# A four-layer attention kernel: hand-assigned buffers, strided layer B weights, norms on ScalarE and a moved overflow check

## The chip, the cores and the metric

The program runs on one core of a Trainium2 chip. The metric is the device time of one execution in microseconds, as the median of several runs. One execution of each kernel is also recorded by the hardware profiler; all profile lines below come from such a record. Engines are named as in the profile: PE (TensorE matmul) with PEld (its weight loads), DVE (VectorE), ACT (ScalarE), POOL (GpSimd) and SP (SyncE, which issues nearly all transfers here).

## The reference

Input is a sequence of 2048 tokens with 512 features in bf16. Four residual layers follow each other, A, B, A, B, each `x = x + layer(layernorm(x))`, with 32 heads of 16 features. Both A layers share their weights, and so do both B layers.

```python
# layer A: linear attention
pq, pk = q @ w_phi, k @ w_phi                    # per head, 16 x 16
phi_q = concat(softmax(pq), softmax(-pq))        # phi_k from pk likewise
kv = einsum("bhsf,bhsd->bhfd", phi_k, v); z = phi_k.sum(s)
o = (phi_q @ kv) / (phi_q @ z + 1e-6)
out = o @ wo
# layer B: each token looks at 8 tokens, 0, 2, .. 14 positions back
logits = q . k[pos - 2 * w] * 16 ** -0.5         # masked ahead of the start
o = softmax(logits) @ v[pos - 2 * w]
out = o @ wo
```

## The kernel before, in words

Tokens lie on partitions for the normalization and in blocks of 512 (b = 0 to 3) on the free axis elsewhere. x stays in SBUF through all layers, as four tiles of 128 x 4 x 512. `w_phi` is folded into the q and k weights at the start (`s_fold`, WA).

**Normalization.** Mean and variance come from `bn_stats` for the first layer (L379) and later from sums that the residual step leaves behind: the residual is added either on PE, by one more matmul with the identity (L411), and copied out by ACT (L418), or on DVE (L421); ACT squares x for the sum of squares (L428). DVE applies the normalization (L334, `xn`), PE transposes (L348), ACT or DVE copies out (`xnT`, L146 or L148).

**Layer A.** `s_a1`: k and v by matmul (L469, L481), exp of k and -k on ACT (L475, `Ek`), sums over features as a tree on DVE (L501, L505, L509, L513), reciprocals on ACT, one multiplication on DVE (L521), and the sum over tokens on PE (L530). `s_a2`: q (L559) and its exps (L565, `Eq`). `s_akv`, `s_a3`, `s_a4`: the masked kv matrices (L600, L607), denominators, a broadcast of rho either by PE (L654, L660) or by a round trip through DRAM (L669, L676, L680), the product (L705) and the output projection with the residual (`s_out`, L408).

**Layer B.** `s_b1` computes q, k, v with features as rows and tokens as columns (L727), four groups c of 128 features for each. In these groups each head's features are split over the four groups, so the columns of the weights are taken in the order (h, dl) for each c. Before, GpSimd makes a permuted copy WB of the raw weights for it (L278). ACT or DVE copies the results out (K, QT, V). V is spread by transfers from SBUF to SBUF into `Vg` (L779): 16 for each block. `s_b2`: products of q with eight shifted views of k on DVE (L808, `prod`), sums over features by PE (L815), exps on ACT (L822, `E`, whose row sums go into `stE`), denominators (L831, L836, L838, `rden`, sums into `stR`) and the normalized weights (L843, `PT`). `s_b3`: products with the shifted v on DVE (L868, `pav`), sums by PE (L875), output projection (L408) and residual. In the last layer the result is stored from there (L432).

**The check.** The exps are taken without a maximum. Whether this is safe is checked: norms of the folded weights (`s_bound`: squares on GpSimd L300, column sums on PE L305, comparison and count on DVE L309), the sums in `stE` and `stR` (L893, L895), all added up over partitions by PE (L900) and compared on DVE (L902, L904). Every engine loads the result `fl` (L906) and branches over a second, general program (L1541) that is there for the case that it isn't safe; it is not run here.

**Order and buffers.** Each engine works through its queue in order. The queues' order is written out by hand: `_ORDER` is a table of base-36 numbers, each naming a thread (a stage and an engine), and `run()` takes the next step of that thread. `_CHOICE` has a digit for each step that can run on either of two engines (which engine copies out; whether the residual is added on PE). Tiles come from pools: `big` with 8 buffers (Ek, Vg, prod, pav), `med` with 16 (xn, xnT, Eq, K, QT, V, oT and others), `t2` with 6, and `ps` with 8 PSUM banks. A pool hands its buffers out in turn, so a new tile waits until the tile that had the buffer has been read for the last time.

## Time and profile before

| what | value |
|---|---|
| median of 3 runs | 368.34 us (368.2 to 368.52) |
| the profiled execution's own time | 368.67 us |
| its span, first to last instruction | 367.0 us |
| mean granted TensorE clock | 0.989 |
| GpSimd busy | 18.8 us |
| transfers | 30.65 MB, mean 84 GB/s |

The profile is read in this way: the page gives busy time and share of the span for each engine; a group line gives source line, engine, operation, tiles written <- read, shapes and count, then busy us and mean ns, then the idle time of the engine before these instructions and what ended it. A timeline line gives start and duration in us of a run of like instructions, and in brackets the idle time before it. A chain line gives start, duration and what the end of the program was waiting for. A line of a single source line gives durations in ns as minimum/median/maximum and the first and the last start. Durations of matmuls are modelled and overlap, so PE is judged by the distance between starts.

### The profile page before, as it was taken

To read this page: it belongs to the slowest core of one execution; us is meant where nothing else is said; L and a number is where in the kernel's file an instruction comes from. 1 tells how busy PE (TensorE), PEld (TensorE's weight loads), DVE (VectorE), ACT (ScalarE), POOL (GpSimd) and SP (SyncE) were. 2 spreads that over 40 slices of the span, in tenths; PEclk is the share of its full clock that TensorE was granted. 3 is DMA by queue.
4 is the path that set the end of the run, shared out by engine and by line. 5 is a ranking of instruction groups with operands and counts; after the bars stand their busy time and mean duration, and the time that the engine had idled before them with its cause. 6 is when DMAs were issued, how large, how long until landed. Compare 5 with 4: busy or idle time off the path is not lost.

```text
span 367.0 us, 7333 instructions
## 1 busy us (share of the span) xinstructions
PE 336.5 (92%) x2868; PEld 162.5 (44%) x2868; DVE 318.5 (87%) x460; ACT 272.9 (74%) x622; POOL 18.8 (5%) x40
## 2 busy tenths in 40 slices
PE   1999899899999999999997999997999999998591
PEld 0645456644544443443433556643454444433130
DVE  7689987699689999999997959797799999995972
ACT  2579798487866979789897998487678889775250
POOL 3070400300000000000000000000000000000000
PEclk9999999999999999999999999999999999999897
DMA  7930000013400799309940000015204796489513
GB/s 232 350 94 0 3 0 2 4 46 92 110 1 0 125 152 158 55 29 174 189 84 0 2 0 3 2 51 133 65 0 85 134 158 97 91 157 167 118 53 127
DMA packets 17242, 30.65 MB, mean 84 GB/s; under 512 B 4272, under 2 KB 11952, under 8 KB 17200
## 3 DMA queue, kind: packets, MB, share of 16 engines
q1 hardware_dynamic: 16672, 30.09, 39.6%
q8 instruction: 24, 0.39, 0.5%
q14 instruction: 18, 0.15, 0.2%
q10 hardware_dynamic: 528, 0.02, 0.1%
HBM read 10.50 MB, written 2.36 MB: 35 GB/s over the span
## 4 chain that ended last, share of the span: by engine, by line
PE 64%; DVE 16%; ACT 9%; DMA 6%; issue 2%; SPq 1%; DVEq 0%; ACTq 0%
PE ps L727 23%; PE ps L408 13%; PE ps L815 4%; PE ps L481 4%; PE ps L348 4%; PE ps L875 3%; ACT Ek L475 3%; DMA Vg<-V 3%; PE ps L705 3%; PE ps L469 3%; DVE Ek L521 2%; ACT Eq L565 2%; DVE pav L868 2%; PE ps L530 2%; DVE Eq L660 2%
## 5 line engine op out<-in xcount | busy, mean ns | idle before, releaser
L727 PE MATMUL ps<-xnT,WB 128*128 128x512 bf16 x384 | 88.0, 379 | 0.0
L808 DVE TENSOR_TENSOR prod<-QT,K 128x4096 bf16<-128x4096 bf16 x32 | 72.0, 2288 | 2.1 <-ACT K L148 1.7
L868 DVE TENSOR_TENSOR pav<-PT,Vg 128x4096 bf16<-128x4096 bf16 x32 | 71.4, 2288 | 0.3
L727 PEld LDWEIGHTS <-WB 128*128 128x128 bf16 x384 | 36.4, 98 | 48.0 <-issue 5.9
L148 ACT CAST oT<-ps 128x512 bf16<-128x512 f32 x58 | 33.1, 602 | 17.6 <-PE ps L875 11.5
L408 PEld LDWEIGHTS <-oT 128*128 128x128 bf16 x256 | 23.8, 99 | 33.7 <-issue 7.4
L475 ACT ACTIVATE Ek<-ps 128x512 bf16<-128x512 f32 x64 | 34.5, 625 | 3.3 <-PE ps L469 3.3
L565 ACT ACTIVATE Eq<-ps 128x512 bf16<-128x512 f32 x64 | 34.1, 632 | 2.5 <-PE ps L559 1.5
L408 PE MATMUL ps<-WoB,oT 128*128 128x512 bf16 x128 | 32.7, 390 | 0.0
L469 PE MATMUL ps<-WA,xnT 128*128 128x512 bf16 x128 | 31.1, 379 | 1.6 <-DVE vaug L146 1.3
L481 PE MATMUL ps<-WA,xnT 128*128 128x512 bf16 x128 | 32.0, 390 | 0.0
L408 PE MATMUL ps<-WoA,oT 128*128 128x512 bf16 x128 | 31.3, 380 | 0.0
L559 PE MATMUL ps<-xnT,WA 128*128 128x512 bf16 x128 | 30.5, 379 | 0.2 <-ACT Eq L565 0.2
L428 ACT ACTIVATE sqd<-x 128x512 bf16<-128x512 bf16 x48 | 30.0, 632 | 0.8 <-DVE x L421 0.5
L421 DVE SCALAR_TENSOR_TENSOR x<-ps,x 128x512 bf16<-128x512 f32 x37 | 24.4, 685 | 5.8 <-PE ps L408 5.7
L348 PE MATMUL ps<-ident,xn 128*128 128x128 bf16 x256 | 19.7, 225 | 8.4 <-DVE xn L334 8.4
L875 PE MATMUL ps<-pav,indAV 128*32 128x512 bf16 x256 | 18.9, 391 | 7.0 <-DVE pav L868 5.2
L148 ACT COPY xnT<-ps 128x1024 bf16<-128x1024 bf16 x21 | 21.1, 1035 | 3.3 <-PE ps L348 3.3
L348 PEld LDWEIGHTS <-xn 128*128 128x128 bf16 x256 | 16.6, 100 | 15.4 <-DVE xn L334 10.0
L521 DVE TENSOR_TENSOR Ek<-Ek,rk 128x4096 bf16<-128x4096 bf16 x8 | 18.3, 2289 | 5.5 <-ACT rk L518 5.5
L148 ACT CAST QT<-ps 128x512 bf16<-128x512 f32 x30 | 17.5, 586 | 5.6 <-PE ps L727 5.3
L418 ACT ACTIVATE x<-ps 128x512 bf16<-128x512 f32 x27 | 15.8, 598 | 7.6 <-PE ps L411 7.4
(118 smaller groups left out, 468.3 us busy)
## 6 DMA issues: line engine op xcount, KB each, us to landing
Vg<-V SPq DMA_DIRECT2D x128, 131.5 KB, 4.7
Prho<-rd SPq DMA_DIRECT2D x8, 512.0 KB, 4.7
out_dram<-x SPq DMA_DIRECT2D x8, 256.0 KB, 2.5
x<-in_A_x_dram SPq DMA_DIRECT2D x3, 512.0 KB, 8.3
wbraw<-in_B_wqkv_dram SPq DMA_DIRECT2D x3, 512.0 KB, 8.8
wraw<-in_A_wqkv_dram SPq DMA_DIRECT2D x2, 512.0 KB, 6.4
x<-in_A_x_dram SPq DMA_DIRECT2D x4, 128.0 KB, 2.5
WA<-in_A_wqkv_dram SPq DMA_DIRECT2D x1, 512.0 KB, 4.4
```

Of the source, the lines that this page charges most:

```text
L148: self.nc.scalar.copy(out=out, in_=in_)
L348: nc.tensor.transpose(U["pt", t // 2][:, (t % 2 * NB + c) * P:(t % 2 * NB + c + 1) * P], self.xn[key, b][:, t, c * P:(c + 1) * P], self.id ...
L408: nc.tensor.matmul(y[:], lhsT=oT[:, c, t * P:(t + 1) * P], rhs=Wo()[:, c, :], start=(c == 0), stop=(c == NB - 1 and not onpe))
L428: nc.scalar.activation(out=sqd[:], in_=xb[:, t, :], func=ACT.Square, accum_out=T["ss"][:, t:t + 1])
L469: nc.tensor.matmul(pk[:], lhsT=xnT[:, t, k, :], rhs=self.WA[:, k, D:2 * D], start=(k == 0), stop=(k == NB - 1))
L475: nc.scalar.activation(out=T["E"][:, t, s, :], in_=T["k", t][:], func=ACT.Exp, scale=1.0 - 2.0 * s)
L481: nc.tensor.matmul(pv[:], lhsT=xnT[:, t, k, :], rhs=self.WA[:, k, 2 * D:3 * D], start=(k == 0), stop=(k == NB - 1))
L559: nc.tensor.matmul(pq[:], lhsT=self.WA[:, k, hb * P:(hb + 1) * P], rhs=xnT[:, :, k, :], start=(k == 0), stop=(k == NB - 1))
L565: nc.scalar.activation(out=self.Eq[L, b][s][:, :, hb, :], in_=T[hb][:].rearrange("p (t i) -> p t i", t=4), func=ACT.Exp, scale=1.0 - 2.0 * s)
L727: nc.tensor.matmul(pp[:], lhsT=self.WB[:, k, i, c, :], rhs=xnT[:, :, k, :], start=(k == 0), stop=(k == NB - 1))
L808: nc.vector.tensor_tensor(out=pr[:], in0=QT[:, c:c + 1, :].to_broadcast([P, NW, TB]), in1=win, op=ALU.mult)
L868: nc.vector.tensor_tensor(out=pv[:], in0=PT[:].unsqueeze(1).to_broadcast([P, NB, 2, TB]), in1=vw, op=ALU.mult)
```

## The change

It has four parts, and with them both tables are written anew.

1. **Buffers by hand.** Each pool is split into pools of one buffer, and `_SLOTS` names the buffer of every tile in the order in which tiles are made. The numbers of buffers stay 8, 16, 6 and 8. `wT` and the two tiles of `Eq` are made one step later.
2. **Layer B's weights.** WB is loaded as it lies in DRAM; group c takes every fourth column from c on. The rows of WoB are loaded in the matching order, in runs of one row where they were runs of four. GpSimd's twelve copies are gone.
3. **Weight norms.** ACT squares the q and k parts of WA with a running sum (one sum for each partition); GpSimd's squares, PE's eight matmuls and DVE's two counts are gone. The bound is now on the sum over the whole matrix.
4. **The flag.** It becomes three scheduled steps: counts (DVE), total (PE), decide (DVE), with a sign and a threshold for each of four numbers; the load of `fl` by every engine stays at the end.

`_ORDER` and `_CHOICE` are new, so that nearly every queue differs; by the built queues PE adds 21 residuals, where it added 27.

```diff
-COLN2_MAX = 3.0
+FRO2_MAX = 2.9
+_BUFS = {"big": 8, "med": 16, "t2": 6, "ps": 8}
 _ORDER = """
-4 1r 4 0 5 4 0 1 4 4 6 6 0 0 2 0 2 3 n o n 7 16 16 p n q n r n n t 15 8 8 8 8 16 16 1a u u s 13 8 19 9 8 8 8 8
+0 8l 0 4 4 1f 1 n 4 0 0 n 0 5 4 o 2 4 6 6 p n 2 n q u 3 u n n t 8 8 8 8 9 15 15 s 16 7 15 w 8 15 8 8 8 9i 17 v
...
+_SLOTS = {
+    "big": (
+        "01234567012437437561327546107534610751205462034162034571620345712630416325725472014751432"
+    ),
...
-        self.bigp = e(tc.tile_pool(name="bigp", bufs=8))
+        self.bigp = e(tc.tile_pool(name="bigp", bufs=1))
...
+    def slot(self, kind):
+        k = self.ntile[kind]
+        self.ntile[kind] = k + 1
+        return kind + _SLOTS[kind][k]
...
-        return self.bigp.tile([P] + shape, BF16, name=name, tag="big")
+        return self.bigp.tile([P] + shape, BF16, name=name, tag=self.slot("big"))
...
-        self.WB = const.tile([P, NB, 3, NB, P], BF16, name="WB")
+        self.WB = const.tile([P, NB, 3 * D], BF16, name="WB")
...
         def ld(i):
-            T[i] = self.med([NB, D], "wbraw")
-            nc.sync.dma_start(out=T[i][:], in_=wbv[:, :, i * D:(i + 1) * D])
-
-        def cp(i, m):
-            nc.gpsimd.tensor_copy(
-                out=self.WB[:, m, i, :, :].rearrange("p c (h dl) -> p c h dl", dl=4),
-                in_=T[i][:, m, :].rearrange("p (h c dl) -> p c h dl", c=NB, dl=4))
+            wbv = self.B_wqkv.rearrange("(m p) c -> p m c", p=P)
+            nc.sync.dma_start(out=self.WB[:, :, i * D:(i + 1) * D], in_=wbv[:, :, i * D:(i + 1) * D])
 
         def wo(c):
-            wo_v = self.B_wo.rearrange("(h c q) n -> c h q n", c=NB, q=4)
+            wo_v = self.B_wo.rearrange("(h q c) n -> c h q n", c=NB, q=4)
...
         def sq(qk):
-            T[qk] = self.med([NB, D], "sq")
-            w = self.WA[:, :, qk * D:(qk + 1) * D]
-            nc.gpsimd.tensor_tensor(out=T[qk][:], in0=w, in1=w, op=ALU.mult)
-
-        def mm(qk):
-            T["p", qk] = pn = self.ps()
-            for m in range(NB):
-                nc.tensor.matmul(pn[:], lhsT=self.ones[:], rhs=T[qk][:, m, :], start=(m == 0), stop=(m == NB - 1))
-
-        def cmp(qk):
-            okm = self.t2([D], "okm")
-            nc.vector.tensor_scalar(out=okm[:], in0=T["p", qk][:], scalar1=COLN2_MAX, scalar2=None,
-                                    op0=ALU.is_le, op1=ALU.add, accum_out=self.okc[:, qk:qk + 1])
+            junk = self.med([NB, D], "sq")
+            nc.scalar.activation(out=junk[:], in_=self.WA[:, :, qk * D:(qk + 1) * D], func=ACT.Square,
+                                 accum_out=self.okc[:, qk:qk + 1])
...
-                nc.tensor.matmul(pp[:], lhsT=self.WB[:, k, i, c, :], rhs=xnT[:, :, k, :],
+                nc.tensor.matmul(pp[:], lhsT=self.WB[:, k, i * D + c:(i + 1) * D:NB], rhs=xnT[:, :, k, :],
...
+    def s_flag(self):
+        nc, add = self.nc, self.step
+        T = {}
+
+        def counts():
+            junk = self.sm([24], "junk", F32, 1)
+            nc.vector.tensor_scalar(out=junk[:, 0:16], in0=self.stE[:], scalar1=SUM_E_MAX, scalar2=None,
+                                    op0=ALU.is_le, op1=ALU.add, accum_out=self.okc[:, 2:3])
+            nc.vector.tensor_scalar(out=junk[:, 16:24], in0=self.stR[:], scalar1=SUM_R_MAX, scalar2=None,
+                                    op0=ALU.is_le, op1=ALU.add, accum_out=self.okc[:, 3:4])
+            T["okb"] = self.sm([4], "okb", BF16, 1)
+            nc.vector.tensor_tensor(out=T["okb"][:], in0=self.okc[:], in1=self.sgn[:], op=ALU.mult)
+
+        def total():
+            T["p"] = self.ps()
+            nc.tensor.matmul(T["p"][:, 0:4], lhsT=self.ones[:], rhs=T["okb"][:], start=True, stop=True)
+
+        def decide():
+            ok = self.sm([4], "ok", F32, 1)
+            nc.vector.tensor_tensor(out=ok[:], in0=T["p"][:, 0:4], in1=self.thr[:], op=ALU.is_ge)
+            tot = self.sm([1], "tot", F32, 1)
+            nc.vector.tensor_reduce(out=tot[:], in_=ok[:], axis=AX.X, op=ALU.add)
+            self.fl = self.sm([1], "fl", I32, 1)
+            nc.vector.tensor_scalar(out=self.fl[:], in0=tot[:], scalar1=4.0, scalar2=None, op0=ALU.not_equal)
+
+        add("flag", "DVE", counts)
+        add("flag", "PE", total)
+        add("flag", "DVE", decide)
```

Line numbers of the changed kernel are higher: 13 more in the norms and transposes (L334 becomes L347, L421 becomes L434), 15 more in layer B (L727 becomes L742, L808 becomes L823, L868 becomes L883), and 29 more for the helper that copies (L146 becomes L175, L148 becomes L177).

149 lines of the change are left out of this document (76 added, 73 removed).

## The prediction, made before the changed kernel ran

> **What bounds the kernel now.** I read the page first, then busy time by stage, then the DVE timeline, the chain of waits and single source lines where something stood out. The page gives the length and the load of each engine:
>
> ```profile
> span 367.0 us, 7333 instructions
> PE 336.5 (92%) x2868; PEld 162.5 (44%) x2868; DVE 318.5 (87%) x460; ACT 272.9 (74%) x622; POOL 18.8 (5%) x40
> ```
>
> Two engines near 90% can be one bottleneck or two that take turns. The busy time by stage (columns: stretch, its length, then PE, PEld, DVE, ACT, POOL busy us with counts) tells:
>
> ```profile
> 20.00:82.00 62.00, 58.31 (x692) 33.53 (x690) 53.83 (x91) 49.09 (x106) 12.62 (x14) 1.00 0.04 10
> 82.00:110.00 28.00, 28.00 (x155) 13.57 (x154) 23.41 (x49) 20.30 (x46) 0.32 (x2) 1.00 0.28 72
> 110.00:200.00 90.00, 88.16 (x629) 37.38 (x628) 87.87 (x98) 75.70 (x178) 0.79 (x4) 1.00 0.58 98
> 200.00:270.00 70.00, 66.81 (x723) 36.52 (x722) 56.10 (x106) 55.94 (x137) 0.00 (x0) 1.00 0.13 33
> 270.00:330.00 60.00, 60.00 (x433) 25.47 (x431) 58.68 (x53) 49.71 (x115) 0.00 (x0) 1.00 0.60 110
> 330.00:355.00 25.00, 19.02 (x127) 6.43 (x127) 20.82 (x17) 10.97 (x24) 0.00 (x0) 0.93 0.61 106
> ```
>
> In the layer A stages (20 to 82, 200 to 270) PE leads and DVE has 8 and 14 us free. In the layer B stages (110 to 200, 270 to 330) PE and DVE are both full. There is slack in one late place: from 330 to 355 PE is idle for 6.0 us and DVE for 4.2. That stretch on DVE (start, duration, instruction, and in brackets the idle time before it with its releaser):
>
> ```profile
> 324.10 6.69 DVE L808 TENSOR_TENSOR prod<-QT,K 128x4096 bf16<-128x4096 bf16 x3
> 333.46 0.17 DVE L893 TENSOR_SCALAR_CACHE_REDUCE junk<-stE 128x16 f32<-128x16 f32 x1 [2.68 <-ACT E L822]
> 333.56 0.69 DVE L843 TENSOR_TENSOR PT<-E,rden 128x1024 bf16<-128x1024 bf16 x1
> 335.37 0.16 DVE L895 TENSOR_SCALAR_CACHE_REDUCE junk<-stR 128x8 f32<-128x8 f32 x1 [1.12 <-ACT rden L838]
> 335.57 0.17 DVE L898 CAST okb<-okc 128x4 bf16<-128x4 f32 x1
> 335.78 4.49 DVE L868 TENSOR_TENSOR pav<-PT,Vg 128x4096 bf16<-128x4096 bf16 x2
> 342.99 11.10 DVE L868 TENSOR_TENSOR pav<-PT,Vg 128x4096 bf16<-128x4096 bf16 x5
> ```
>
> The last `prod` ends at 330.79. From 335.78 to 354.09 DVE runs eight `pav` and a PT without a hole, and everything after it hangs on them. Between lie 4.99 us with 0.69 of use (PT): the flag's counts stand in DVE's queue there, and they want the sums of the last block that ACT makes (E, then rden), while PT and `pav` behind them want the block before it. So the two counts hold up the engine that sets the tail. The chain of waits blames a transfer here:
>
> ```profile
> 335.05 6.43 DMA Vg<-V
> 341.55 1.44 issue
> 342.99 2.30 DVE pav L868
> ```
>
> but the `pav` of 342.99 starts the moment its predecessor ends; the transfer had landed 1.5 us earlier. It is second in line, not first.
>
> **The change, part by part.** *Flag counts.* DVE's queue before, from the last products to the end of the kernel's main path (prod: logits products; pav: attention times V; okb, tot, fl: flag):
>
> ```order
> L808 TENSOR_TENSOR prod<-QT,K 128x4096 x8
> L893 TENSOR_SCALAR junk,okc<-stE 128x16
> L843 TENSOR_TENSOR PT<-E,rden 128x1024
> L895 TENSOR_SCALAR junk,okc<-stR 128x8
> L898 CAST okb<-okc 128x4
> L868 TENSOR_TENSOR pav<-PT,Vg 128x4096 x2
> L843 TENSOR_TENSOR PT<-E,rden 128x1024
> L868 TENSOR_TENSOR pav<-PT,Vg 128x4096 x6
> ```
>
> DVE's queue in the same place now, and on to the flag's end:
>
> ```order
> L823 TENSOR_TENSOR prod<-QT,K 128x4096 x6
> L858 TENSOR_TENSOR PT<-E,rden 128x1024
> L883 TENSOR_TENSOR pav<-PT,Vg 128x4096 x2
> L858 TENSOR_TENSOR PT<-E,rden 128x1024
> L883 TENSOR_TENSOR pav<-PT,Vg 128x4096 x6
> L911 TENSOR_SCALAR junk,okc<-stE 128x16
> L913 TENSOR_SCALAR junk,okc<-stR 128x8
> L916 TENSOR_TENSOR okb<-okc,sgn 128x4
> L175 CAST oT<-ps 128x512
> L434 SCALAR_TENSOR_TENSOR x_86<-ps,x_86 128x512
> ```
>
> The counts have moved behind all eight `pav`; PT follows the products at once. At most 4.99 - 0.69 = 4.3 us go. If the Vg transfers do not start earlier, only the 1.5 us between landing and use can go. The transfers' buffers are freed by `prod` and `pav`, which run earlier too, and the last two `pav` use a Vg tile 16 us into the run, so I take 3.5. After the last `pav` the three counts (some 0.5 us) lie on DVE while PE sums `pav` and ACT copies oT, so they cost nothing; without that cover, 0.5.
>
> *End of the program.* The title's "ahead of the tail" holds for the counts alone. These are the last DVE rows now (ok and thr: the new comparison against thresholds):
>
> ```order
> L434 SCALAR_TENSOR_TENSOR x_86<-ps,x_86 128x512 x3
> L924 TENSOR_TENSOR ok<-ps,thr 128x4
> L926 TENSOR_REDUCE tot<-ok 128x1
> L928 TENSOR_SCALAR fl<-tot 128x1
> L935 TENSOR_LOAD fl
> L1572 COMPARE_AND_BRANCH
> ```
>
> Three small steps follow the last residual instead of two. Every engine loads fl and branches on it after that, and PE's branch is the long one:
>
> ```profile
> 355.81 3.80 PE L408 MATMUL ps<-WoB,oT 128*128 128x512 bf16 x16
> 357.05 3.28 DVE L421 SCALAR_TENSOR_TENSOR x<-ps,x 128x512 bf16<-128x512 f32 x5 [2.36 <-PE ps L408]
> 360.43 0.15 DVE L904 TENSOR_SCALAR fl<-tot 128x1 int32<-128x1 f32 x1
> L1541 PEldq COMPARE_BRANCH  x1: 3913/3913/3913, 361.5 to 361.5; - x1
> ```
>
> PE is done at 359.6 and could branch 1.0 us earlier if fl were there; it is not, so nothing is won and one 0.15 step is added: +0.2.
>
> *GpSimd's work.* The twelve copies into WB and the two squarings leave GpSimd:
>
> ```profile
> 17.68 5.29 POOL L278 COPY WB<-wbraw 128x512 bf16<-128x512 bf16 x9 [14.08 <-DMA wbraw<-in_B_wqkv_dram]
> 18.42 2.41 DVE L334 TENSOR_SCALAR xn<-x,q,rstd 128x512 bf16<-128x512 bf16 x4
> 35.70 0.41 DVE L334 TENSOR_SCALAR xn<-x,q,rstd 128x512 bf16<-128x512 bf16 x1
> 37.52 4.15 POOL L300 TENSOR_TENSOR sq<-WA 128x2048 bf16<-128x2048 bf16 x1 [12.65 <-ACT WA L148]
> 38.25 3.97 DVE L505 TENSOR_TENSOR s<-s 128x1024 bf16<-128x1024 bf16 x1
> L505 DVE TENSOR_TENSOR s<-s x8: 685/692/3970, 32.9 to 226.1; 128x1024 bf16<-128x1024 bf16 x8
> 43.33 1.02 PE L469 MATMUL ps<-WA,xnT 128*128 128x512 bf16 x4 [1.29 <-DVE vaug L146]
> ```
>
> One DVE sum took 3.97 us where its median is 0.69, and ended as the squaring did (41.67): 3.3 us of DVE lost. Four normalizations beside the copies took 2.41 where 4 x 0.41 = 1.64 was due: 0.8. What reaches the end is between nothing (later work of ACT fills the hole) and those 4.1; PE waited 1.3 behind the long sum, so I take 1.3 for it, and 0.8 for the normalizations, with which the first PE work begins.
>
> *Weight norms.* Eight matmuls L305 and two DVE counts L309 go; two squarings of 128x2048 join ACT's queue at the head of layer B. What stands there on ACT now (xnT: the transposed input of the next block; sqd: its sums of squares):
>
> ```order
> L342 ACTIVATE rstd<-lnv 128x4
> L177 CAST V<-ps 128x512
> L324 ACTIVATE sq,okc<-WA 128x2048 x2
> L177 COPY xnT<-ps 128x1024 x2
> L441 ACTIVATE sqd,ss<-x_86 128x512
> L177 CAST QT<-ps 128x512
> ```
>
> The squarings wait for nothing, but xnT and what follows wait for them. The nearest rows, with those for the other counted work:
>
> ```profile
> L428 ACT ACTIVATE sqd<-x x48: 613/630/662, 85.3 to 305.3; 128x512 bf16<-128x512 bf16 x48
> L148 ACT COPY xnT<-ps 128x1024 bf16<-128x1024 bf16 x21 | 21.1, 1035 | 3.3 <-PE ps L348 3.3
> 94.09 6.04 PE ps L727 x28
> L309 DVE TENSOR_SCALAR_CACHE_REDUCE okm<-ps x2: 685/685/685, 69.1 to 95.1; 128x512 bf16<-128x512 f32 x2
> L421 DVE SCALAR_TENSOR_TENSOR x<-ps,x x37: 680/685/693, 84.4 to 359.6; 128x512 bf16<-128x512 f32 x37
> 20.76 0.67 DVE L146 COPY xnT<-ps 128x1024 bf16<-128x1024 bf16 x1
> 17.36 0.70 DVE L146 CAST vaug<-ps 128x512 bf16<-128x512 f32 x1 [1.57 <-PE ps L481]
> ```
>
> A square of 512 columns is 0.63 us, a copy of 1024 is 1.04, so one of 2048 lies between 2 x 1.04 = 2.1 and 4 x 0.63 = 2.5; both, 4.2 to 5.0. ACT is free for 28.0 - 20.3 = 7.7 us in the stretch where they land. PE has about nine groups of four matmuls in its queue that need no xnT, worth 7.8 us, so most is covered; I take +0.5, bounds 0 and +5.0 (all of it, if the banks that ACT must empty run out).
>
> *Work that changes engine.* 28 matmuls of 512 columns in 6.04 us are 0.216 each. L305 is worth 8 x 0.216 = 1.7 on PE. The number of residuals added on PE falls from 27 to 21: 6 x 0.216 = 1.3 off PE, 6 x 0.69 = 4.1 onto DVE; two counts of 0.69 leave it. Copies out of PSUM change sides too: by the two queues DVE has two more of 512 columns and two fewer of 1024, 0.70 and 0.67 each, none in sum. So PE loses 3.0 us and DVE gains 2.7. Where PE alone leads, that is -3.0; in the B stages, where DVE has 2.1 of 90 and 1.3 of 60 us free, it is +2.7 at worst. Some of both: -1.0, nearer to PE's end, since the chain of waits runs mostly on PE.
>
> *Weights with stride 4.* The load of 128 weights now takes every fourth column:
>
> ```profile
> L727 PEld LDWEIGHTS <-WB x384: 95/98/99, 93.7 to 326.0; 128*128 128x128 bf16 x192
> 100.14 0.89 PE ps L348 x16
> ```
>
> No row has a strided load. A packed one takes 98 ns beside a matmul that streams for 216; and sixteen transposes of 128 columns, each with a load of its own, pass in 0.89 us, 56 ns apiece. A load can thus grow 2.2 times by the one row, almost four times by the other, before PE notices. Bounds: 0, and for four times 98 ns, 384 x (392 - 216) = 67.6 us. I take 0, as the cover is wide. The Trainium skill ("SBUF — State Buffer", Specifications (TRN2)) says that SBUF has lines of 16 bytes, that two accesses to a line are needed for full bandwidth and that each crossing to a new line pays a penalty. A stride of four bf16 makes exactly two accesses per line but four times the crossings, so the rule's first half gives no cost and its second half the slower rival below; no run here shows it yet.
>
> *Buffers and order.* All queues are rewritten. Waits for buffers are there before:
>
> ```profile
> SPq L779 <- PE ps L815: 32.2, 5, 25.3
> L408 PE MATMUL ps<-WoB,oT x128: 377/379/634, 147.4 to 359.2; 128*128 128x512 bf16 x128
> ```
>
> The first is the Vg transfers held until PE has read the `prod` in their buffer. But a wait of SP's queue is not one of PE or DVE, so the sum holds no gain for it. PE's own holes bound what a better order could add: 1.8 in 110 to 200, 3.2 in 200 to 270, 3.7 in 20 to 82 of which 1.3 is counted, 7.4 in all; an estimate of six tenths of it is 4.5. A worse order can lose as well; nothing in the rows bounds that. WB's three transfers stand where those of its raw copy stood. WoB's four, now in shorter runs, are spread in SP's queue among the transfers of rho and Vg; WoB is first read at 147.4, long after, so they cost nothing while a transfer lands within tens of microseconds.
>
> Sum against the profiled execution of 368.67 (span 367.0 and 1.7 around it): -3.5 - 1.3 - 0.8 - 1.0 + 0.5 + 0.2 = -5.9, so 362.8. The three timed runs have a median 0.3 lower, 368.34, so 362.4.
>
> **The rivals.** *DVE takes it back.* The B stages are bound by DVE, the gains of GpSimd's absence lie in A stages that ACT fills anyway: -3.5 + 2.7 + 0.5 + 0.2 = -0.1, so 368.2. For it: 87.87 of 90 us busy. Against: PE is as full. *Weight loads show.* At 2.5 times the time, 245 ns, PE steps at 245 instead of 216: 384 x 0.029 = 11 us, so 373.5 with the gains kept; at four times 430. It decides from 216 ns on. For it: every load of these 384 is in the fullest stages; against: the 56 ns. *The order gains more.* With hand-set buffers the holes above close as well: 362.4 - 4.5 = 357.9. For it: the 32.2 us of waiting for buffers; against: nothing in these rows shows that they made PE's holes.
>
> **How the numbers follow.** Forecast 0.63: with its two main terms, tail and GpSimd, at their good ends together (-4.3 and -4.1 for -3.5 and -2.1) 359.6, at their bad ends (-1.5 and 0) 366.5. More from the order 0.13, down to 356.5 with half of those 2.8 us. DVE takes it back 0.15, 366.7 to 369.7 as its 2.7 may be 1.2 or 4.2 (4.1 without the counts that leave). Weight loads 0.09. A measurement here tells 0.2%, 0.7 us, from no change. The DVE rival lies on both sides of that, a third each: faster 0.63 + 0.13 + 0.05 = 0.81; same 0.05; slower 0.05 + 0.09 = 0.14. The range 356.5 to 368.0 leaves out the weight loads, over half of the DVE rival and a little at the low end, 0.2 in all.
>
> **What would show it.** Right: in the changed profile PT follows the last product within 0.3 us and the eight `pav` run unbroken; L518 (the sum) is 0.7 us every time; weight loads of L742 stay near 100 ns; steps of L742 stay at 216. Wrong: `pav` waiting on Vg in the tail by over 1.5 us, PE waiting on xnT behind the squarings, or loads above 216 ns.

## The result and the profile after

The changed kernel takes 352.84 us (median of 4 runs, 352.35 to 353.28) against 368.43 (368.2 to 368.67): a ratio of 0.9576, 95% interval 0.956 to 0.9593, 15.6 us less. The forecast was 6.0 less: right in sign and in several steps, and wrong in size, outside its range. Below, differences between runs are ratios to the kernel before on the same chip times 368.4, since that kernel's median lies between 368.15 and 368.84 by chip. The 95% intervals of single runs reach 0.5 to 1.8 us to either side, those of a difference of two runs up to 2.4; what lies within its interval isn't told from nothing.

The page of the changed kernel:

```profile
span 350.6 us, 7264 instructions
PE 329.1 (94%) x2829; PEld 166.5 (47%) x2854; DVE 316.4 (90%) x470; ACT 272.4 (78%) x613; POOL 4.2 (1%) x32
```

PE's first matmul starts at 8.92 and its last ends at 343.44 (before: 8.19 and 359.61). Of these 334.5 us it is busy for 329.1, so its holes are 5.4; before, 351.4 - 336.5 = 14.9. But this page has 2829 matmuls for 2854 weight loads, one of which stands before each matmul: 25 matmuls are missing from the record, and each leaves an apparent hole of about 0.05 us, some 1.3 in all (before, none is missing). So of the 16.4 us of span about 10.8 are holes that closed, 6.1 are busy time that went and 0.2 lie behind PE's end, less 0.7 for the later start. Of the 6.1, 14 fewer matmuls are worth 14 x 0.216 = 3.0 and a stretch of lowered clock in the old tail 1.7 (below); the rest isn't broken down. Busy time by stage (columns as in the prediction; the cuts lie at the same places of the program, not at the same times):

```profile
20.00:75.00 55.00, 54.46 (x603) 30.73 (x604) 45.83 (x82) 48.15 (x104) 0.62 (x4) 1.00 0.01 3
102.00:196.00 94.00, 93.30 (x648) 42.17 (x652) 90.50 (x104) 81.34 (x191) 0.34 (x2) 1.00 0.49 97
196.00:258.00 62.00, 60.72 (x706) 35.21 (x711) 55.93 (x110) 50.21 (x119) 0.15 (x1) 1.00 0.08 20
320.00:344.00 24.00, 21.90 (x159) 8.13 (x153) 22.85 (x21) 13.54 (x28) 0.00 (x0) 1.00 0.84 155
```

PE is now nearly full in these stages, in the A stages too; in the tail it is still idle for 2.1 of 24 us. DVE's tail (start, duration, instruction):

```profile
310.95 8.89 DVE L823 TENSOR_TENSOR prod<-QT,K 128x4096 bf16<-128x4096 bf16 x4
319.81 0.69 DVE L858 TENSOR_TENSOR PT<-E,rden 128x1024 bf16<-128x1024 bf16 x1
320.60 4.50 DVE L883 TENSOR_TENSOR pav<-PT,Vg 128x4096 bf16<-128x4096 bf16 x2
325.01 0.69 DVE L858 TENSOR_TENSOR PT<-E,rden 128x1024 bf16<-128x1024 bf16 x1
325.80 13.30 DVE L883 TENSOR_TENSOR pav<-PT,Vg 128x4096 bf16<-128x4096 bf16 x6
```

PT follows the last product at once and the `pav` run unbroken, as forecast: 19.3 us from the last product to the last `pav`, where it was 23.3. The rows for the other steps (one source line each: ns as minimum/median/maximum), and ACT and PE at the head of layer B:

```profile
L518 DVE TENSOR_TENSOR s<-s x8: 681/692/693, 33.9 to 215.7; 128x1024 bf16<-128x1024 bf16 x8
L742 PEld LDWEIGHTS <-WB x384: 110/113/135, 86.3 to 315.2; 128*128 128x128 bf16 x192
L324 ACT ACTIVATE sq<-WA x2: 1901/1906/1912, 95.5 to 97.4; 128x2048 bf16<-128x2048 bf16 x2
100.77 7.93 PE L742 MATMUL ps<-xnT,WB 128*128 128x512 bf16 x36
```

No sum is held up any more. A strided load takes 113 ns where a packed one took 98, and PE's step is unchanged: (7.93 - 0.38) / 35 = 0.216. A squaring takes 1.9 us on ACT, and PE runs through behind it.

### The profile page after: what moved, and what is told of

Same layout as the page of the kernel before. It is cut to its first block, busy times and chain, and to the rows that moved or that the text cites. A ratio compares the mean times of both kernels' runs of the same rounds, so it can differ in the third digit from the quotient of the medians.

```text
span 350.6 us, 7264 instructions
## 1 busy us (share of the span) xinstructions
PE 329.1 (94%) x2829; PEld 166.5 (47%) x2854; DVE 316.4 (90%) x470; ACT 272.4 (78%) x613; POOL 4.2 (1%) x32
## 4 chain that ended last, share of the span: by engine, by line
PE 74%; ACT 10%; DVE 7%; DMA 3%; issue 3%; SPq 2%; DVEq 0%; ACTq 0%
PE ps L742 23%; PE ps L421 11%; PE ps L494 7%; PE ps L482 6%; PE ps L361 4%; PE ps L543 4%; PE ps L572 4%; PE ps L830 3%; PE ps L720 3%; ACT Eq L580 3%; PE ps L890 3%; DVE pav L883 2%; SPq L794 2%; DVE Eq L675 2%; DMA wraw<-in_A_wqkv_dram 2%
## 5 line engine op out<-in xcount | busy, mean ns | idle before, releaser
L742 PE MATMUL ps<-xnT,WB 128*128 128x512 bf16 x384 | 90.0, 380 | 0.0
L883 DVE TENSOR_TENSOR pav<-PT,Vg 128x4096 bf16<-128x4096 bf16 x32 | 72.3, 2288 | 1.0 <-PE ps L424 0.2
L823 DVE TENSOR_TENSOR prod<-QT,K 128x4096 bf16<-128x4096 bf16 x32 | 72.0, 2287 | 0.2
L742 PEld LDWEIGHTS <-WB 128*128 128x128 bf16 x384 | 41.8, 114 | 42.7 <-issue 7.4
L421 PEld LDWEIGHTS <-oT 128*128 128x128 bf16 x256 | 23.7, 98 | 33.1 <-issue 3.5
L177 ACT CAST oT<-ps 128x512 bf16<-128x512 f32 x52 | 29.9, 601 | 5.0 <-PE ps L890 3.2
L421 PE MATMUL ps<-WoB,oT 128*128 128x512 bf16 x123 | 31.6, 380 | 0.4
L421 PE MATMUL ps<-WoA,oT 128*128 128x512 bf16 x119 | 30.6, 379 | 1.2 <-DVE oT L175 0.4
L482 PE MATMUL ps<-WA,xnT 128*128 128x512 bf16 x124 | 30.5, 379 | 0.3 <-issue 0.2
L494 PE MATMUL ps<-WA,xnT 128*128 128x512 bf16 x122 | 30.1, 379 | 0.3
L434 DVE SCALAR_TENSOR_TENSOR x<-ps,x 128x512 bf16<-128x512 f32 x43 | 28.3, 685 | 1.4 <-PE ps L421 1.0
L177 ACT COPY xnT<-ps 128x1024 bf16<-128x1024 bf16 x24 | 24.2, 1032 | 3.8 <-PE ps L361 3.7
L177 ACT CAST QT<-ps 128x512 bf16<-128x512 f32 x31 | 18.0, 598 | 8.1 <-PE ps L742 8.0
L675 DVE TENSOR_TENSOR Eq<-ps,Eq 128x512 bf16<-128x512 f32 x32 | 19.9, 683 | 1.1 <-PE ps L669 1.0
L177 ACT CAST V<-ps 128x512 bf16<-128x512 f32 x32 | 18.8, 600 | 2.5 <-PE ps L742 2.4
L177 ACT CAST K<-ps 128x512 bf16<-128x512 f32 x29 | 16.8, 595 | 4.8 <-PE ps L742 4.8
L431 ACT ACTIVATE x<-ps 128x512 bf16<-128x512 f32 x21 | 12.4, 598 | 10.0 <-PE ps L424 10.0
```

The source lines that it names most:

```text
L177: self.nc.scalar.copy(out=out, in_=in_)
L421: nc.tensor.matmul(y[:], lhsT=oT[:, c, t * P:(t + 1) * P], rhs=Wo()[:, c, :], start=(c == 0), stop=(c == NB - 1 and not onpe))
L482: nc.tensor.matmul(pk[:], lhsT=xnT[:, t, k, :], rhs=self.WA[:, k, D:2 * D], start=(k == 0), stop=(k == NB - 1))
L494: nc.tensor.matmul(pv[:], lhsT=xnT[:, t, k, :], rhs=self.WA[:, k, 2 * D:3 * D], start=(k == 0), stop=(k == NB - 1))
L742: nc.tensor.matmul(pp[:], lhsT=self.WB[:, k, i * D + c:(i + 1) * D:NB], rhs=xnT[:, :, k, :], start=(k == 0), stop=(k == NB - 1))
L823: nc.vector.tensor_tensor(out=pr[:], in0=QT[:, c:c + 1, :].to_broadcast([P, NW, TB]), in1=win, op=ALU.mult)
```

## The experiments

Three theories. *Tail and parts*: the gain is that of the moved counts, of GpSimd's absence and of PE's lost matmuls, each larger than forecast. *Order*: the new queues close PE's holes by themselves. *Buffers*: the hand-set buffers do it.

### Which part gave how much

**tail_only.** The kernel before; its flag steps, which stood behind the block that fixes the order (so that the framework chose their place), go to the end inside it.

```diff
         with tc.manual_schedule(engines=_ORDERED):
             fast.run()
+            fast.flag_steps()
         redo = fast.flag()
```

> The kernel before, with one change: the flag's steps (L893 to L904) stand inside the hand-written order, behind all else, instead of outside of it; so DVE does the two counts after the last pav. Everything before the last product should be as before. Theory 'the tail gives what was forecast': 3.5 us less, some 364.9. Theory 'the tail gives more than forecast' (the whole 5.4 us by which the stretch from the last product to PE's last matmul shrank between the two kernels): some 363.

Measured 362.69; ratio 0.9844 (0.9811 to 0.9877), 5.7 us less: the larger size. The stretch from the last product to the end of PE's last output matmul, before and here (columns as above; the last but two is PE's granted clock):

```profile
330.80:359.70 28.90, 22.82 (x150) 7.80 (x148) 22.58 (x21) 12.30 (x25) 0.00 (x0) 0.94 0.57 110
```

```profile
328.90:352.40 23.50, 21.16 (x149) 7.53 (x147) 22.11 (x17) 12.33 (x25) 0.00 (x0) 1.00 0.69 136
```

5.4 us less (the profiled execution also reached its last product 1.8 us earlier, which the edit doesn't explain). From the last product to the last `pav` it is 23.3 us before and, by DVE's rows here, 19.0:

```profile
320.06 8.89 DVE L808 TENSOR_TENSOR prod<-QT,K 128x4096 bf16<-128x4096 bf16 x4
334.66 13.30 DVE L868 TENSOR_TENSOR pav<-PT,Vg 128x4096 bf16<-128x4096 bf16 x6
```

So 4.3 is the wait in DVE's queue, all of it. The other 1.1 lie between the last `pav` and PE's last output matmul: in the kernel before, PE waits for `pav` twice and then runs at about half clock for a while (PE's timeline, then windows):

```profile
343.13 0.62 PE L875 MATMUL ps<-pav,indAV 128*32 128x512 bf16 x8 [2.19 <-DVE pav L868]
345.34 1.05 PE L875 MATMUL ps<-pav,indAV 128*32 128x512 bf16 x8 [1.59 <-DVE pav L868]
340.00:343.00 3.00, 0.61 (x8) 0.12 (x8) 3.00 (x4) 0.56 (x1) 0.00 (x0) 1.00 1.01 151
343.00:346.00 3.00, 1.28 (x16) 0.26 (x16) 3.00 (x3) 0.00 (x0) 0.00 (x0) 0.85 0.57 175
346.00:349.00 3.00, 3.00 (x12) 0.97 (x8) 3.00 (x2) 2.05 (x4) 0.00 (x0) 0.58 0.00 0
```

At 0.85 and 0.58 PE loses 0.15 x 3 + 0.42 x 3 = 1.7 us of work, and from 345.3 on it has no hole in which to make them good. In tail_only the clock stays at 1.00 there.

**parts_old_order** and **parts_old_order_2.** Parts 2, 3 and 4 on the old order, choice and pools. The two differ in the place of ScalarE's squarings (thread names for the numbers of the table):

```diff
 a4_01o.ACT a4_02.F100ev b1_00v.PE a4_01o.F75res b1_00v.F54ev b1_00k.PE a4_01o.ACT b1_00k.PE b1_00q.PE
-bound.ACT bound.ACT
 b1_00q.PE b1_00k.F50ev b1_00v.PE a4_01o.ACT a4_01o.DVE a4_01o.ACT
...
 b1_00v.F55ev
+bound.ACT
...
 b1_01k.F82ev
+bound.ACT
```

> Parts 2, 3 and 4 of the change (strided weights, norms on ScalarE, flag in steps) on the old order, the old choice of engines and the ordinary pools; the two squarings stand in ACT's queue where the second count stood, at the head of the first layer B. Theory 'the order gave the rest': the gain is that of the tail (4 to 5.4), of PE's eight matmuls (1.7) and of GpSimd's absence (0 to 2.1), 7 at most 9, so 359.5 to 362. Theory 'the parts gave it, since removing GpSimd's work and PE's work closes PE's holes by itself': within 2 us of the changed kernel, 353 to 355.

> As the run of parts 2 to 4 on the old order, but with ScalarE's two squarings placed some 8 us later, where ACT idled for 4.3 us in eight pieces, behind the transposed input of the next block instead of ahead of its statistics. Theory 'that kernel lost 2.6 us because PE waited for what stood behind the squarings': 361 to 362, with PE's idle time between 90 and 105 us gone. Theory 'the loss came from the strided loads or the missing GpSimd copies': 364 as before.

The first: 364.27, ratio 0.9892 (0.9856 to 0.9928), slower than the tail alone. PE stood still behind the squarings (ACT, then PE):

```profile
94.19 1.90 ACT L299 ACTIVATE sq<-WA 128x2048 bf16<-128x2048 bf16 x1
96.08 1.90 ACT L299 ACTIVATE sq<-WA 128x2048 bf16<-128x2048 bf16 x1
99.95 1.37 PE L334 MATMUL ps<-ident,xn 128*128 128x128 bf16 x16 [2.59 <-ACT oT L148]
```

The second: 361.78, ratio 0.9801 (0.9753 to 0.985), so where the squarings stand is worth 3.4 us. Well placed, parts 2 and 3 give 1.6 beyond the tail, which the interval of that difference (2.2 to either side) doesn't tell from nothing. Its PE works from 8.28 to 352.61 and is busy for 332.1 of it: 12.2 us of holes remain, some 1.4 of them apparent, since 28 matmuls are missing from this record.

**all_but_hand_buffers.** The changed kernel with ordinary pools; every engine's order is the same.

```diff
-        self.bigp = e(tc.tile_pool(name="bigp", bufs=1))
+        self.bigp = e(tc.tile_pool(name="bigp", bufs=8))
...
-        return self.bigp.tile([P] + shape, BF16, name=name, tag=self.slot("big"))
+        return self.bigp.tile([P] + shape, BF16, name=name, tag="big")
```

> The changed kernel with part 1 undone alone: pools of 8, 16, 6 and 8 buffers that the framework fills, the same order on every engine. Theory 'hand-set buffers matter': 2 to 6 us slower than the changed kernel, 355 to 359, with new holes on PE that end when a buffer comes free. Theory 'any assignment does, the order decides': within 1 us of it, 352 to 354.

353.58, ratio 0.958 (0.9542 to 0.9618): within 0.7 us of the changed kernel. The buffers set by hand do nothing that can be told here. Against parts_old_order_2 order and choice differ, and the later making of `wT` and `Eq` that came with part 1: 8.1 us. PE works from 9.98 to 344.68, busy for 330.8: 3.9 us of holes (no matmul is missing here) where there were 12.2 less 1.4, so some 6.9 closed. Where they closed (parts_old_order_2, then all_but_hand_buffers):

```profile
60.00:70.00 10.00, 7.93 (x274) 7.43 (x271) 5.06 (x13) 5.54 (x14) 0.00 (x0) 0.91 0.01 3
190.00:200.00 10.00, 8.18 (x60) 3.37 (x61) 8.18 (x12) 7.81 (x19) 0.00 (x0) 1.00 0.00 0
200.00:260.00 60.00, 56.61 (x672) 31.98 (x675) 49.47 (x94) 48.43 (x119) 0.00 (x0) 1.00 0.15 38
```

```profile
60.00:70.00 10.00, 9.77 (x218) 6.35 (x219) 6.68 (x17) 6.99 (x17) 0.30 (x2) 1.00 0.01 2
190.00:200.00 10.00, 9.91 (x73) 4.48 (x72) 9.98 (x20) 9.92 (x24) 0.00 (x0) 1.00 0.00 0
200.00:260.00 60.00, 59.04 (x692) 33.78 (x691) 53.55 (x102) 47.93 (x115) 0.15 (x1) 1.00 0.08 21
```

1.8, 1.7 and 2.4 us, in the places that the prediction listed as PE's own holes. Most of them are three waits of PE for DVE (parts_old_order_2); the fourth row is the nearest to the first in all_but_hand_buffers:

```profile
67.38 0.40 PE L640 MATMUL ps<-rho,indB 32*128 32x128 bf16 x16 [2.07 <-DVE rho L633]
196.74 1.05 PE L861 MATMUL ps<-pav,indAV 128*32 128x512 bf16 x16 [1.77 <-DVE x L407]
251.74 1.67 PE L691 MATMUL ps<-Eq,R 128*128 128x512 bf16 x7 [1.88 <-DVE Eq L646]
66.21 0.40 PE L669 MATMUL ps<-rho,indB 32*128 32x128 bf16 x16 [0.23 <-DVE rho L662]
```

The first and the third end with what PE reads next. The second ends with a residual, which reads a PSUM bank and makes nothing that these matmuls read, so by its row it is a wait for a bank. None of the three is left in the new order, with ordinary pools; which single moves close them, no run shows. The first wait also cooled PE: behind it the clock is at half from 68.1 to 71.5 (0.91 in the row above), 1.7 us of work, and at 1.00 in the new order.

**order_alone** and **order_and_tail.** The kernel before with the new order and choice; in the second the flag stands at the end as well. GpSimd's work, for which the new table has no place, goes in like this:

```diff
 loadB.SP
+loadB.POOL loadB.POOL loadB.POOL loadB.POOL
...
 a1_03k.PE
+bound.POOL
...
 a4_00o.ACT
+bound.POOL
...
-bound.ACT bound.ACT
+bound.PE bound.DVE bound.PE bound.DVE
```

> The kernel before with the new order and the new choice of engines alone: ordinary pools, packed weights by GpSimd's copies (behind the loads), GpSimd's squares, PE's column sums and DVE's counts as before (squares where they stood, sums and counts where the new order has ScalarE's squarings), flag outside of the order as before. Theory 'the order gave the rest': it gains what the parts don't, 7 to 9 us, so 359 to 361; with PE bound from end to end its 1.7 us of column sums cost in full. Theory 'the parts gave it': 366 to 369.

> The kernel before with the new order and choice, and the flag's steps at the end of the order: parts 2 and 3 undone (GpSimd copies and squares, PE's column sums and DVE's counts are there), ordinary pools. The tail is worth some 5.8 us on the old order (the run of that alone). Theory 'order and tail add up, and GpSimd's work takes the rest': 368.0 - 5.8 = 362, with the first half of the program (up to the last output projection of layer 2) 8 us or more longer than in the changed kernel and the second half equal to it. Theory 'the order needs the tail's edit': 354 to 357.

368.02, ratio 0.9969 (0.995 to 0.9989), and 365.08, ratio 0.9894 (0.9849 to 0.9939). The order gives 1.1 by itself, and with the tail 3.9, less than the tail alone on the old order. So order and parts do not add up: on top of the tail, the order gains 8.1 with parts 2 and 3 in place and, without them, gains nothing (it loses 1.8, with an interval of 2.0 to either side). Something that those parts remove is in the new order's way.

### What is in its way

**undo_strided_weights** and **undo_norms.** The changed order and choice on ordinary pools, with part 2 undone, and with part 3 undone; GpSimd's steps stand in the order as in the two runs above.

```diff
-                nc.tensor.matmul(pp[:], lhsT=self.WB[:, k, i * D + c:(i + 1) * D:NB], rhs=xnT[:, :, k, :],
+                nc.tensor.matmul(pp[:], lhsT=self.WB[:, k, i, c, :], rhs=xnT[:, :, k, :],
```

```diff
-            nc.scalar.activation(out=junk[:], in_=self.WA[:, :, qk * D:(qk + 1) * D], func=ACT.Square,
-                                 accum_out=self.okc[:, qk:qk + 1])
+            nc.gpsimd.tensor_tensor(out=T[qk][:], in0=w, in1=w, op=ALU.mult)
```

> The changed order, norms on ScalarE and the flag as changed, but weights of layer B as before: loaded raw, copied into order by twelve GpSimd copies, read packed. Ordinary pools, which alone cost 0.7 us. Theory 'GpSimd's copies cost what they lie beside': the normalizations and sums that run during a copy take longer, 1 to 3 us in all, so 354.5 to 357. Theory 'strided loads cost something': they are 114 ns where packed ones were 98, so this kernel would be equal or faster, 352 to 353.6. Theory 'the copies hold up layer B' : above 358.

> The changed order, strided weights and the flag behind all pav, but the norms as before: two squarings of 128x2048 on GpSimd, eight matmuls of column sums on PE and two counts on DVE; ordinary pools. Theory 'each GpSimd squaring stops one DVE instruction for its whole length, and PE is the bound': 1.7 for PE's eight matmuls, up to 3.3 for each squaring by what DVE does then, so 355.3 to 362; in the run of the order alone the second squaring fell on rho (3.33 us instead of 0.41) and PE then waited on the chain behind it. Theory 'norms are nothing': 353 to 354.

353.36, ratio 0.9571 (0.9526 to 0.9616): strided or copied weights make no difference that can be told (2.2 to either side). 365.35, ratio 0.9886 (0.9835 to 0.9937): the norms, done as before, cost 11.3 us in the new order. GpSimd's second squaring, DVE's rho under it, and PE later (timeline; then two windows):

```profile
75.44 3.60 POOL L295 TENSOR_TENSOR sq<-WA 128x2048 bf16<-128x2048 bf16 x1 [5.80 <-PE ps L700]
75.99 3.33 DVE L642 TENSOR_TENSOR rho<-rS,Ds 128x256 bf16<-128x256 f32 x1
94.93 1.51 PE L700 MATMUL ps<-Eq,R 128*128 128x512 bf16 x5 [2.17 <-DVE Eq L675]
96.24 3.99 PE L722 MATMUL ps<-xnT,WB 128*128 128x512 bf16 x11
92.00:96.00 4.00, 1.83 (x9) 0.80 (x8) 2.31 (x5) 0.00 (x0) 0.00 (x0) 0.97 0.23 50
96.00:100.00 4.00, 4.00 (x13) 1.51 (x11) 4.00 (x10) 3.78 (x11) 0.00 (x0) 0.60 0.06 12
```

PE waits for `Eq`, which is multiplied by rho after its round trip through DRAM, and then eleven matmuls take 3.99 us at a clock of 0.60.

**plus_gp_squares, plus_pe_sums, gp_square_in_gap, gp_square_on_rho.** Added to all_but_hand_buffers, with results that nobody reads: the two squarings; eight matmuls and two counts; one squaring in DVE's longest wait; one squaring where undo_norms has its second, on rho.

```diff
+        def gsq(qk):
+            gp = self.med([NB, D], "sq")
+            w = self.WA[:, :, qk * D:(qk + 1) * D]
+            nc.gpsimd.tensor_tensor(out=gp[:], in0=w, in1=w, op=ALU.mult)
...
+            for m in range(NB):
+                nc.tensor.matmul(pn[:], lhsT=self.ones[:], rhs=self.WA[:, m, qk * D:(qk + 1) * D],
+                                 start=(m == 0), stop=(m == NB - 1))
...
+                w = T["E"][:, :, 0, :]
+                nc.gpsimd.tensor_tensor(out=gp[:], in0=w, in1=w, op=ALU.mult)
```

> The changed kernel with ordinary pools (353.6) and, added, two squarings of 128x2048 on GpSimd whose results nobody reads, at the places where the run with the norms undone had them; nothing else. Theory 'a GpSimd squaring stops DVE wherever it lands, and the chain behind it does the rest': 5 to 10 us slower, 358.5 to 363.5, the larger part of the 12 us of that run. Theory 'the 12 us came from PE's column sums and DVE's counts': within 1 us of 353.6.

> The changed kernel with ordinary pools (353.6) and, added, eight matmuls of 512 columns and two DVE counts of 128x512 at the head of layer B, which nobody reads; they wait for nothing but a PSUM bank. Theory 'PE is the bound from end to end': 8 x 0.216 = 1.7 us slower, 355.3, and 1 us more if the counts' 1.4 us on DVE show too. Theory 'there is slack at that place': within 0.5 us of 353.6. If it is over 3 us, the column sums carry much of the 12 us of the run with the norms undone.

> The changed kernel with ordinary pools (353.6) and, added, one GpSimd squaring of 128x2048 that nobody reads, made of the last Ek behind DVE's last multiplication of layer 1, so that it falls into the 3.8 us (58.6 to 62.4) in which DVE waits for PE's sum over tokens. The old order had its second squaring in such a place. Theory 'a squaring costs what DVE does under it': within 0.5 us of 353.6, since DVE has nothing to do. Theory 'GpSimd's work costs by itself (buffers, the port, PE's reads)': 1 to 3 us more.

> The same with the one squaring where the run with the norms undone had its second one, at 75.4 us, on DVE's rho (0.41 us there without it, 3.33 with it), from which a transfer through DRAM and PE's output projection hang. Theory 'a squaring costs what DVE does under it': 2 to 4 us more than 353.6, most of the 4.0 us that the two squarings cost together. If it is under 1 us, it was the first one, on the normalizations at 26 us, that cost.

| run | us | ratio (95%) | beyond all_but_hand_buffers |
|---|---|---|---|
| plus_gp_squares | 357.54 | 0.9694 (0.9647 to 0.9742) | 4.2 |
| plus_pe_sums | 355.86 | 0.9654 (0.9601 to 0.9707) | 2.7 |
| gp_square_in_gap | 353.25 | 0.9601 (0.9578 to 0.9624) | 0.8 |
| gp_square_on_rho | 356.02 | 0.968 (0.9655 to 0.9705) | 3.7 |

The place decides. First the squaring in the gap, with DVE beside it; then the one on rho:

```profile
57.45 3.60 POOL L566 TENSOR_TENSOR sq<-Ek 128x2048 bf16<-128x2048 bf16 x1 [25.96 <-DVE Ek L534]
61.15 0.47 DVE L621 TENSOR_TENSOR ZM<-ps,maskR 128x24 bf16<-128x24 f32 x3 [3.78 <-PE ps L543]
```

```profile
72.79 3.60 POOL L330 TENSOR_TENSOR sq<-WA 128x2048 bf16<-128x2048 bf16 x1 [11.31 <-ACT Eq L587]
73.55 3.12 DVE L669 TENSOR_TENSOR rho<-rS,Ds 128x256 bf16<-128x256 f32 x1
```

DVE waits those 3.78 us without a squaring too, so the first one costs nothing that can be told (0.8, with an interval of 1.6 to either side; the medians differ by -0.3). The one on rho costs 3.7, nearly all that the two of plus_gp_squares do. The kernel before had its second squaring in just such a wait:

```profile
65.17 3.60 POOL L300 TENSOR_TENSOR sq<-WA 128x2048 bf16<-128x2048 bf16 x1 [23.50 <-ACT Eq L565]
66.66 0.47 DVE L600 TENSOR_TENSOR ZM<-ps,maskR 128x24 bf16<-128x24 f32 x3 [4.15 <-PE ps L530]
```

The single costs sum to 6.9; undo_norms lost 11.3. The 4.4 between them have an interval of some 3.5 to either side. That they are the chain from squares to sums to counts, with the halved clock, is argued and not shown; another place for the squares might cost less.

**counts_early.** The changed kernel with the counts where they stood.

```diff
+flag.DVE
 b2_13.DVE
+b2_12.ACT flag.DVE
 b3_13.DVE b3_13.PE b3_13.DVE b3_13.PE
-b2_12.ACT
```

> The changed kernel with the two counts back where they stood: the first ahead of the PT that follows the last product, the second ahead of the pavs. Theory 'the counts hold the tail': 4 to 5.5 us slower than the changed kernel, 357 to 358.5, with PT 2 to 3 us behind the last product. Theory 'the new order feeds the sums earlier, so the counts would not wait': 353 to 354.

356.06, ratio 0.9661 (0.9612 to 0.971), 3.1 us slower than the changed kernel: below the range that was expected, while the tail's edit was worth 5.7 on the old order. The counts wait as before:

```profile
321.72 0.17 DVE L911 TENSOR_SCALAR_CACHE_REDUCE junk<-stE 128x16 f32<-128x16 f32 x1 [2.24 <-ACT E L837]
323.63 0.16 DVE L916 TENSOR_SCALAR_CACHE_REDUCE junk<-stR 128x8 f32<-128x8 f32 x1 [1.13 <-ACT rden L853]
```

From the last product (319.48) to the last `pav` (342.54) it is 23.1 us, 3.8 more than in the changed kernel. So the mechanism holds; the difference to 5.7 is barely outside of the intervals and stays open.

### Order and choice

**old_choice** (new order, old `_CHOICE`) and **new_choice_old_order** (the kernel before, new `_CHOICE`).

```diff
-    "0110111000000011100001000000011001000000000000100011000000000111010010110000000000100000000000100000"
...
```

> The changed kernel with ordinary pools (353.6) and the old choice of engines on the new order: 27 residuals on PE where the new choice has 21, and the old sides for the copies out of PSUM. Theory 'PE is the bound, so six matmuls are 1.3 us, and the order does the rest': 354.5 to 357. Theory 'the choice of engines is what the order's gain consists of': 360 or more.

> The kernel before with the new choice of engines alone, on the old order: six residuals fewer on PE and the copies on the new sides. The old choice on the new order cost 24.5 us. Theory 'each choice fits its own order': 375 or more. Theory 'the new choice is better in itself': 362 to 367.

378.09, ratio 1.0244 (1.0193 to 1.0295), and 401.41, ratio 1.088 (1.0848 to 1.0912). Each choice fits its own order and costs over 20 us on the other. My guess of some microseconds for the first was far off; that a copy on the other engine stands in another queue, ahead of other work, is the likely reason and wasn't taken apart. In the second PE's granted clock averages 0.969 where the kernel before has 0.989, so a part of its loss is clock.

**second_half_new.** parts_old_order_2 with the new order and choice for the last two layers alone; steps of layer 2 are taken earlier where a step of layer 3 needs them.

```diff
+later = lambda x: bool(re.match(r"(a1_1|a2_1|akv1|a3_1|a4_1|b1_1|b2_1|b3_1|flag)", x))
+it = iter([x for x in new if later(x)])
+seq = [next(it) if later(x) else x for x in old]
```

> The better kernel with parts 2 to 4 on the old order (361.8), with the new order and choice for the last two layers alone; the steps of the first two keep their old order and choice. Every run with the new order took 7.2 us less from the last output projection of layer 2 to the last product than every run with the old one (119.8 against 127.0), whatever the other parts. Theory 'the second half's gain is the order's own and stands by itself': 361.8 - 7.2 = 354.6, to 356 with what the seam costs. Theory 'it comes from work that the new order does ahead, in holes of the first half': 359 to 362.

370.68, ratio 1.0074 (1.005 to 1.0098): 10 us slower than its base, and both theories fall. Between 160 and 220 us, where the layers overlap, PE is busy for 50.2 us here and for 57.9 in its base. Waits cooled PE as well: its clock is at half from 219.9 to 226.8. So the 7.2 us that every run with the new order saves in the second half is no gain that this half brings by itself. That a part of it is work that the first half has already done is argued and not shown, since the seam costs too.

**dve_probe.**

```diff
+            w = self.WA[:, 0:2, 0:D]
+            nc.vector.tensor_tensor(out=w, in0=w, in1=w, op=ALU.max)
```

> The changed kernel with ordinary pools (353.6) and, added, six DVE operations of 0.7 us each (maximum of a part of WA with itself, 128x1024, WA being no longer needed there), behind every other one of the products of the last layer: 4.1 us of DVE work in the stretch where DVE idles by about 1.2 us. Theory 'PE alone is the bound': under 1 us. Theory 'PE and DVE are both full in layer B': 3 to 4.5 us.

355.19, ratio 0.9643 (0.9627 to 0.9659), 2.3 us for 4.1 us of DVE work, between the two theories (the interval is 1.5 to either side). Without the probe, from 250 to 322 us, DVE is busy for 70.5 of 72 and PE for 71.7; with it, for 71.6 and 70.0. DVE had 1.5 us to spare, and 4.1 - 1.5 = 2.6 is about what was lost: the two engines are nearly even there.

### A faster version

**decide_early.**

```diff
+flag.DVE
 b3_12o.F266res b3_10o.F208res b3_10o.SP b3_13o.F299res b3_13o.SP b3_12o.F267res b3_12o.SP b3_12o.F268res b3_12o.F269res
-flag.DVE
 b3_12o.SP
```

> The changed kernel (352.8) with one step moved: the flag's comparison, sum and result (three DVE steps) stand ahead of the last four residuals instead of behind them, in DVE's 0.8 us of idle time, so that PE can load the flag and take its branch of 3.8 us as soon as its last matmul is out. Theory 'PE's branch sets the end': 1.0 to 1.2 us less, 351.7. Theory 'the stores or another engine set it': within 0.3 us of 352.8.

351.22 (350.91 to 351.5), ratio 0.9528 (0.9515 to 0.9541), clear of the changed kernel's interval and 1.8 us below it (the profiled spans, 349.8 and 350.6, differ by 0.8): the fastest here, by more than the 1.0 to 1.2 that were expected. PE's branch, in the changed kernel and in this one:

```profile
L1572 PEldq COMPARE_BRANCH  x1: 3797/3797/3797, 345.4 to 345.4; - x1
```

```profile
L1572 PEldq COMPARE_BRANCH  x1: 4637/4637/4637, 341.8 to 341.8; - x1
```

It starts 3.6 us earlier, while PE's last matmuls still run, and ends at 346.4, so that something else ends the program now.

## Why the prediction was wrong

| step | forecast | measured |
|---|---|---|
| tail, with the end of the program | -3.3 | -5.7 (tail_only) |
| GpSimd's absence, weight norms, strided weights, PE's column sums | -1.6 and part of -1.0 | -1.6, 2.2 to either side (parts_old_order_2 less tail_only) |
| order and choice of engines | 0 and part of -1.0 | -8.1 (all_but_hand_buffers less parts_old_order_2) |
| buffers by hand | 0 | -0.1 |

*Buffers and order* is the step that failed: "But a wait of SP's queue is not one of PE or DVE, so the sum holds no gain for it." The buffers gained nothing, as it says, but the sentence stood for the order too, which the sum so put at nothing: it measured 8.1. PE's main holes were three waits for DVE of about 2 us, one of them by its row for a PSUM bank, and the new order closed them, with buffers set by hand or not. By PE's rows of the two runs some 6.9 us are holes that closed, 1.3 are six residuals, and 1.4 are other busy time, about what the clock behind the first wait had cost; 1.7 are lost again, since the first matmul moved from 8.28 to 9.98 (8.92 in the changed kernel, by the same queues). That makes 7.9 for the 8.1. The bound that the prediction set beside it, 7.4 us of PE's holes outside of the tail, was near. I gave it a chance of 0.13 and a price of 4.5, since no row showed that buffers made the holes. It was the order that closed them.

*Tail.* The 3.5 assumed that Vg's transfers would keep part of the 4.3. They were there in time, and the whole 4.3 went. The bound was too low as well: some 1.1 us more went behind the last `pav`, where PE's clock had been lowered behind its waits. The row was in the table of stages from the start (0.93 from 330 to 355), and I read over it.

*GpSimd.* The mechanism was right: the sum is 0.69 every time and the normalizations are 0.41. (The long sum did not end with the squaring at 41.67, as the prediction reads it, but at 38.25 + 3.97 = 42.22: it was held until the squaring was through and then ran.) On the old order the 1.6 that it and the norms were priced at can't be told from the 1.6 measured. What the price left out is the new order: in the old one the second squaring stood in a wait of DVE, and in the new one the norms as before cost 11.3 (undo_norms), a squaring on rho alone 3.7 (gp_square_on_rho).

*Weight norms.* A squaring took 1.9 us, less than the 2.1 to 2.5 of the working. No wait of PE is seen behind them where they stand now; where I first put them in the old order they cost 3.4 us, inside the bounds of 0 to 5.0; PE's reserve of matmuls does not help when the normalization stands behind the squarings.

*Work that changes engine.* plus_pe_sums lost 2.7 (2.4 to either side) for 1.7 us of PE and 1.4 of DVE work, so PE's side seems to count in full; DVE's is free up to 1.5 us in layer B (dve_probe). That makes the -1.0, which lay between the two, look too small; no run measures it apart from the order.

*Weights with stride 4* were right at 0. The Trainium skill's penalty for each crossing to a new line, cited there, would be the 15 ns by which a strided load is longer than a packed one of 98; the rival had 2.5 to 4 times.

*End of the program.* Right: PE's branch starts 2.0 us after its last matmul where it was 1.9. That the flag could come earlier was seen there, and decide_early shows 1.8 for it. (The words "ahead of the tail", which the prediction takes from the title, don't stand in it; the counts went behind the tail's `pav`.)

*The rivals.* "DVE takes it back" and "Weight loads show" are out. "The order gains more" came nearest, at about half the size, but partly by luck: its mechanism, that hand-set buffers close the holes, is out.

## What to carry to other kernels

When a kernel's queues are written anew, list the holes of the engine that sets the pace and put them into the estimate itself, and don't keep them as the bound of a rival: here about two thirds of them closed. A part that gains little alone can be what lets an order work, so price edits together with the order that they permit, and try an order only with its own choice of engines. Look for waits that cool PE: here one of about 2 us could cost 1.7 us of PE's work on top.

## What the runs showed of the hardware

**GpSimd against DVE.** In plus_gp_squares the first squaring runs from 26.01 to 29.61. DVE under it:

```profile
25.78 0.68 DVE L398 BATCH_NORM_STATS2 stat<-x 128x6 f32<-128x512 bf16 x1
26.59 0.66 DVE L398 BATCH_NORM_STATS2 stat<-x 128x6 f32<-128x512 bf16 x1
27.39 3.12 DVE L353 TENSOR_SCALAR xn<-x,q,rstd 128x512 bf16<-128x512 bf16 x3
```

The statistics take 0.66 as ever, while three normalizations worth 1.03 take 3.12: the first of them takes 2.48, to 29.87, just past the squaring's end, and the others then run as usual. So not every DVE instruction is stopped. The Trainium skill ("SBUF — State Buffer", Who interferes with whom) says that a DVE instruction with at most one SBUF input and outside of the two-port modes does not contend with GpSimd, and that the others block for the whole of the first one's instruction. These rows agree, if the normalization runs in a two-port mode, which no row shows; rho, with two SBUF inputs, is of the kind that blocks.

**PE's clock.** It fell to 0.60 after a wait in undo_norms and to 0.58 in the tail before. In parts_old_order PE waited for 2.59 us, and the clock stayed at 1.00 behind it. The Trainium skill ("TensorE: Matmul & The Clock Gate", Part 1) has the clock halve after an idle window of about 3.4 us that runs freely. No single wait ahead of the two drops was that long (2.17 us; 2.19 and 1.59), so shorter waits can do it. The traces show which. In the 20 profiles every stretch at half clock that ends within the record lasts 3.41 us or twice that, and within a run these stretches lie on a grid of that step. Laid on this grid (stretches of undo_norms and parts_old_order; PE's busy us stand behind the length, its clock is the last but two):

```profile
92.35:95.76 3.41, 1.24 (x6) 0.48 (x5) 2.10 (x4) 0.00 (x0) 0.00 (x0) 1.00 0.21 44
95.30:98.71 3.41, 2.06 (x10) 0.87 (x8) 0.00 (x0) 3.38 (x6) 0.17 (x1) 1.00 0.53 154
98.71:102.12 3.41, 2.17 (x21) 1.42 (x22) 2.68 (x6) 2.87 (x6) 0.00 (x0) 1.00 0.01 2
```

In the first PE idles for 2.17 us, and half clock follows. The wait of 2.59 us in parts_old_order falls across a border of the grid, 1.35 us of it in one stretch and 1.24 in the next, and the clock stays. Behind the start it is so in every profile: after a stretch at full clock in which PE idled for 2.06 us or more of the 3.41, the next ran at half clock; after 1.95 or less it did not. Where the grid lies differs from run to run, and so may what a wait does: the four executions of undo_norms have mean clocks of 0.988, 0.989, 0.995 and 0.996.

**Pools.** The description above says that a pool hands its buffers out in turn. No run here shows in which order the framework's pools hand them out; the kernel with such pools and the one with hand-set buffers take the same time within the noise (353.58 and 352.84 us), so here it doesn't matter.
